# Experts: ScalarE's share of conversions and turned rows, issued one step later

## The chip, the cores and the metric

The kernel runs on one core of one Trainium2 chip. The metric is the device time of one launch, in microseconds (us). Of the core's engines five matter: TensorE (PE; its weight loads are listed as PEld), VectorE (DVE), ScalarE (ACT), GpSimd (POOL) and SyncE (SP). Each works through a queue of its own in order. DMAs are issued from the queues of SP, ScalarE and POOL.

## What is computed

Three layers follow each other: a decayed attention, a mixture of eight experts in which every token goes to one expert, and a dense layer with its own nonlinearity.

```python
def _moe_ref(x, modality_id, w_gate, modality_bias, w1, w2):
    ...
    e_idx = np.argmax(logits, axis=1)
    ...
    for e in range(E):
        mask = e_idx == e
        h = np.maximum(x[mask] @ w1[e], 0.0)
        out[mask] = gate_w[mask, None] * (h @ w2[e])

def _moe2_ref(x, w_in, w_out):
    h = x @ w_in
    g = h - np.tanh(h)
    return (g @ w_out).astype(np.float32)
```

There are 4608 tokens of 512 numbers; `w1` and `w2` have 8 x 512 x 1024, `w_in` and `w_out` 512 x 2048. The dense layer's weights come as 64-bit numbers in the kernel's eyes and are turned into 32-bit pairs on the chip.

## The kernel before

All matrix products split each factor into a rounded part and its remainder: ScalarE rounds (a copy into the type fp32r), VectorE subtracts, and TensorE adds three products (high by high, high by low, low by high).

The experts run from 154 to 606 us. Tokens are sorted by expert and cut into 12 *units* of 400; a unit has 8 *steps*, f = 0 to 7, one for each 128 of the 1024 hidden columns. `blocks` emits a step i as follows. TensorE does the first product into `hp` (12 matmuls, line 712). `post` follows: ScalarE rounds the result to `hi` (line 822), VectorE makes the rest `lo` (823); then `split_w` splits two halves of raw weights, ScalarE `wh` (790) and VectorE `wl` (791): the half for this step's second product, and the half for the first product two steps on. Then `prep` emits what else is due, and at last TensorE does the second product of step i - 2 (12 matmuls in four quarters, lines 933 to 935) into four accumulators `acc`. When that was the last of a unit, which is so at f = 1 of the next unit, `finish` has ScalarE copy the four accumulators to `yo` (912). The next unit's second product, at f = 2, starts in the same accumulators.

`prep` fits in two kinds of other work:

- *Turned rows.* The rows of the unit after this one have been gathered by POOL (line 194, 13 gathers a unit). At f = 2 to 5 VectorE turns a group of blocks (`turn_blocks`, line 169) and ScalarE rounds it to `xh` (`split_high`, 182); at f = 3 to 6 VectorE makes `xl` (`split_low`, 186) of the group before.
- *Conversions.* The 32 blocks of `w_in` and `w_out` are taken apart from 64 bit by `conv`, in pieces on VectorE: p0 and p1 (lines 221 to 223), p2 (227, 228), p3 (232, and the sum `cv_a` in 235, which ScalarE then rounds in line 236) and p4 (the low part, 240). Pieces have a price in the table `COST`; every step adds 240 to a credit, turned rows take 69 each, and pieces are issued while the credit pays for them, a p3 as the last of its step, and none at f = 1. With p3 goes the save of the conversion before (line 247, a DMA on ScalarE's queue, for `w_out` only), with p4 the load of the raw block after the next (line 212, on ScalarE's queue too).

So where ScalarE's part of a conversion or of turned rows is emitted, it stands in ScalarE's queue behind this step's `hi` and `wh` and ahead of the next step's.

Of the kernel before, what the change touches and what calls it, by code (L numbers as in the profile page):

```python
# [8 lines left out]
F32 = mybir.dt.float32  # L9
# [50 lines left out]
COST = 126, 111, 138, 69  # L60
# [55 lines left out]
def kernel(tc, A, out):  # L116
    nc = tc.nc
    with ExitStack() as ctx:
# [88 lines left out]
        def conv(cv, src, dh=None, dl=None, dst=None, bufs=2):  # L207
# [22 lines left out]
            def p3():  # L230
                lo, e = d["raw"][:, :, 0], d["e"]
                nc.vector.scalar_tensor_tensor(out=e.bitcast(F32), in0=lo.bitcast(U32), scalar=2.0 ** -52, in1=e.bitcast(F32), op0=ALU.mult, op1=ALU.mult)

                af, ef = (d[n].bitcast(F32) for n in "ae")
                nc.vector.tensor_tensor(out=af, in0=af, in1=ef, op=ALU.add)  # L235
                nc.scalar.copy(out=high(), in_=af)
# [12 lines left out]
            return load, [(COST[0], lambda: (p0(), p1())), (COST[1], p2), (COST[2], p3), (COST[3], p4)], save  # L249

        with tc.manual_schedule():
# [496 lines left out]
            with ExitStack() as c2:  # L748
# [69 lines left out]
                def post(i, hp, ht):  # L818
# [6 lines left out]
                    split_w((i, 1), (i + 2, 0))  # L825
                    load_raw(i + F1)
                    if steps[i] in ((0, 0), (0, 1)):
                        for f in range(3 * i + 3, min(F1, 3 * i + 6)):
                            load_raw(f)

# [9 lines left out]
                def swap():  # L840
# [12 lines left out]
                    for f in range(len(cvs2)):  # L853
                        fill2.extend(cvs2[f][1])
                        if f > 0:
                            fill2[-2] = (fill2[-2][0], lambda a=fill2[-2][1], b=cvs2[f - 1][2]: (a(), b()))
                        if f + 2 < len(cvs2):
                            fill2[-1] = (fill2[-1][0], lambda a=fill2[-1][1], b=cvs2[f + 2][0]: (a(), b()))
                    fill2.reverse()

                def prep(u, f):
# [18 lines left out]
                    if 0 < u < UMIN - 1:  # L880
# [4 lines left out]
                        if f in range(2, 2 + SE):  # L885
                            turn_blocks(v, f - 2, xg[v])
                            split_high(v, f - 2, xg[v])
                            credit[0] -= TURN[0]
# [13 lines left out]
                    while fill2 and fill2[-1][0] <= credit[0] and not (f == 1 and fill2[-1][0] == COST[2]):  # L902
# [6 lines left out]
                def finish(u, acc):  # L909
# [3 lines left out]
                    yos[u] = yo  # L913
                    if u == "t" or u == UMIN - 1:
                        store(u)
# [36 lines left out]
                while fill2:  # L952
                    fill2.pop()[1]()
                total = nc.values_load(nreg[0:1, 0:1], min_val=0, max_val=UMAX)
# [111 lines left out]
```

## Time and profile before

| | |
|---|---|
| time, median of 3 runs | 1397.6 us (1397.01 to 1399.13) |
| the profiled execution | 1397.72 us, of it 1396.0 from the first to the last instruction (the span) |
| TensorE busy | 1358.1 us, 97% of the span |
| VectorE busy | 1048.7 us, 75% |
| ScalarE busy | 695.9 us, 50% |
| POOL busy | 337.3 us, 24% |
| first product of the experts, first matmul | 154.1 us |
| dense layer, first matmul | 606.2 us, 789.8 before the end |

The page lists busy time by engine, the span in 40 slices, DMA queues, the chain of work that ended last and the costliest groups of instructions. Its trace can be asked for waits (who waited for whom), for groups in a stretch, and for instructions in order of time; an instruction's row gives its start, its duration, its line and its tiles, and in brackets the idle time of its engine before it and what ended that.

### The profile page before, as it was taken

To read this page: it belongs to the slowest core of one execution; us is meant where nothing else is said; L and a number is where in the kernel's file an instruction comes from. 1 tells how busy PE (TensorE), PEld (TensorE's weight loads), DVE (VectorE), ACT (ScalarE), POOL (GpSimd) and SP (SyncE) were. 2 spreads that over 40 slices of the span, in tenths; PEclk is the share of its full clock that TensorE was granted. 3 is DMA by queue.
4 is the path that set the end of the run, shared out by engine and by line. 5 is a ranking of instruction groups with operands and counts; after the bars stand their busy time and mean duration, and the time that the engine had idled before them with its cause. 6 is when DMAs were issued, how large, how long until landed. Compare 5 with 4: busy or idle time off the path is not lost.

```text
span 1396.0 us, 22342 instructions
## 1 busy us (share of the span) xinstructions
PE 1358.1 (97%) x8267; PEld 1185.8 (85%) x8267; DVE 1048.7 (75%) x1684; ACT 695.9 (50%) x1232; POOL 337.3 (24%) x381
## 2 busy tenths in 40 slices
PE   8999899999989999999999999999999999999998
PEld 7887798999989999988888888888888888888886
DVE  5766677888888888658878778787787877778775
ACT  3323444444434444446656555555555555565553
POOL 4555353343334444010011100111001110011101
PEclk9999999999999999999999999999999999999999
DMA  9997647444743336634000000000000000000000
GB/s 372 404 332 280 207 151 210 125 132 137 221 126 94 95 94 165 119 128 154 31 31 31 31 1 31 31 31 31 1 31 31 31 31 0 31 31 0 31 1 31
DMA packets 79858, 141.06 MB, mean 101 GB/s; under 512 B 36224, under 2 KB 42944, under 8 KB 79744
## 3 DMA queue, kind: packets, MB, share of 16 engines
q1 hardware_dynamic: 58912, 84.23, 19.3%
q10 hardware_dynamic: 12096, 35.45, 7.2%
q0 software_dynamic: 8736, 19.90, 4.5%
q8 instruction: 66, 1.08, 0.3%
q14 instruction: 48, 0.39, 0.1%
HBM read 133.33 MB, written 39.80 MB: 124 GB/s over the span
## 4 chain that ended last, share of the span: by engine, by line
PE 51%; issue 5%; POOL 0%; POOLq 0%; ACT 0%
PE hp L712 26%; PE acc L1010 8%; PE acc L1012 8%; PE acc L1011 8%; POOL out_dram L1036 0%; POOLq L1062 0%; ACT o L1033 0%; POOL nopt L1035 0%; POOLq L1026 0%; POOLq L1036 0%
## 5 line engine op out<-in xcount | busy, mean ns | idle before, releaser
L983 ACT ACTIVATE eh<-hp 128x512 f32<-128x512 f32 x144 | 86.4, 600 | 293.0 <-PE hp L712 276.0
L712 PE MATMUL hp<-xh,winh 128*128 128x512 f32 x576 | 224.2, 389 | 0.1
L1010 PE MATMUL acc<-wout,hi 128*128 128x512 f32 x576 | 224.2, 389 | 0.0
L1012 PE MATMUL acc<-wout,lo 128*128 128x512 f32 x576 | 224.2, 389 | 0.0
L1011 PE MATMUL acc<-wout,hi 128*128 128x512 f32 x576 | 224.1, 389 | 0.0
L712 PE MATMUL hp<-xh,winl 128*128 128x512 f32 x576 | 224.1, 389 | 0.0
L712 PE MATMUL hp<-xl,winh 128*128 128x512 f32 x576 | 224.1, 389 | 0.0
L985 DVE TENSOR_TENSOR el<-eh,hp 128x512 f32<-128x512 f32 x144 | 99.1, 688 | 156.4 <-ACT eh L984 156.4
L194 POOL DMA_INDIRECT xg<-x_d,idt x130 | 155.6, 1197 | 216.8 <-DVE cv_a L235 70.5
L740 POOL TENSOR_TENSOR xl<-yr,xh 128x512 fp32r<-128x512 f32 x36 | 49.2, 1367 | 429.7 <-ACT xh L739 429.7
L933 PE MATMUL acc<-hi,wh 128*128 128x400 f32 x384 | 132.6, 345 | 16.3 <-ACT yo L912 16.3
L994 DVE SCALAR_TENSOR_TENSOR el<-eh,el 128x512 f32<-128x512 f32 x144 | 128.5, 893 | 15.4 <-DVE el L993 0.5
L712 PE MATMUL hp<-xh,wl 128*128 128x400 f32 x384 | 133.2, 347 | 4.3 <-DVE wl L791 4.0
L791 DVE TENSOR_TENSOR wl<-raw,wh 128x1024 fp32r<-128x1024 f32 (+1 forms) x98 | 117.7, 1202 | 24.4 <-ACT wh L790 23.0
L712 PE MATMUL hp<-xh,wh 128*128 128x400 f32 x384 | 131.7, 343 | 1.2 <-ACT wh L790 0.7
L712 PE MATMUL hp<-xl,wh 128*128 128x400 f32 x384 | 131.5, 342 | 0.8 <-DVE xl L163 0.8
L934 PE MATMUL acc<-lo,wh 128*128 128x400 f32 x384 | 131.3, 342 | 0.0
L935 PE MATMUL acc<-hi,wl 128*128 128x400 f32 x384 | 131.3, 342 | 0.0
L712 PEld LDWEIGHTS hp<-xh,winh 128*128 128x128 f32 x576 | 108.2, 188 | 22.9 <-issue 0.5
L1012 PEld LDWEIGHTS acc<-wout,lo 128*128 128x128 f32 x576 | 108.1, 188 | 22.8 <-DVE lo L989 0.4
L1011 PEld LDWEIGHTS acc<-wout,hi 128*128 128x128 f32 x576 | 108.2, 188 | 22.5
L712 PEld LDWEIGHTS hp<-xh,winl 128*128 128x128 f32 x576 | 108.1, 188 | 22.6
(169 smaller groups left out, 2541.4 us busy)
## 6 DMA issues: line engine op xcount, KB each, us to landing
raw<-in_w_dram SPq DMA_DIRECT2D x91, 512.0 KB
qk<-in_qk_dram SPq DMA_DIRECT2D x36, 512.0 KB
vk<-in_vk_dram SPq DMA_DIRECT2D x36, 512.0 KB
y_d<-yo SPq DMA_DIRECT2D x12, 800.0 KB
yr<-y_d SPq DMA_DIRECT2D x9, 1024.0 KB
raw<-in_wo_dram ACTq DMA_DIRECT2D x16, 512.0 KB
wo_d<-cv_em ACTq DMA_DIRECT2D x16, 512.0 KB
raw<-in_wi_dram ACTq DMA_DIRECT2D x16, 512.0 KB
```

The lines of the kernel that those rows point to most:

```text
L194: nc.gpsimd.indirect_dma_start(out=dst, out_offset=None, in_=x_d[0:NT, :].rearrange("t (q c) -> (t q) c", q=NQ), in_offset=bass.IndirectOf ...
L712: nc.tensor.matmul(out=hp, lhsT=lhs, rhs=rhs, start=j == 0, stop=j == 3 * KD - 1)
L791: nc.vector.tensor_tensor(out=wl[:, 0:n], in0=r, in1=wh[:, 0:n].bitcast(F32), op=ALU.subtract)
L933: nc.tensor.matmul(out=o, lhsT=wh[:, cs], rhs=hi, start=first, stop=False)
L934: nc.tensor.matmul(out=o, lhsT=wh[:, cs], rhs=lo, start=False, stop=False)
L935: nc.tensor.matmul(out=o, lhsT=wl[:, cs], rhs=hi, start=False, stop=last)
L983: nc.scalar.activation(out=u, in_=hp, func=ACTF.Square)
L985: nc.vector.tensor_tensor(out=v, in0=u, in1=hp, op=ALU.mult)
L994: nc.vector.scalar_tensor_tensor(out=v, in0=s, scalar=SQ_C, in1=v, op0=ALU.add, op1=ALU.mult)
L1010: nc.tensor.matmul(out=acc[s], lhsT=hi, rhs=wh, start=first, stop=False)
L1011: nc.tensor.matmul(out=acc[s], lhsT=hi, rhs=wl, start=False, stop=False)
L1012: nc.tensor.matmul(out=acc[s], lhsT=lo, rhs=wh, start=False, stop=last)
```

## The change

ScalarE's rounding of a conversion (now `cast`, line 238), the load of the raw block after the next, the save, and `split_high` are no longer emitted where VectorE's piece is. They are put in a list, `late_act`, and `flush` emits the list in the next step's `post`, behind that step's `hi` and `wh`. At f = 1 of every unit but the first, `flush` is left to `finish`, behind the four `yo`. The cast and the load go with p3, the save with p4 of the same conversion. At f = 1 it is now p4 that isn't issued, where it was p3. No instruction is added or taken away.

```diff
--- before.py
+++ after.py
@@ -233,7 +233,9 @@
 
                 af, ef = (d[n].bitcast(F32) for n in "ae")
                 nc.vector.tensor_tensor(out=af, in0=af, in1=ef, op=ALU.add)
-                nc.scalar.copy(out=high(), in_=af)
+
+            def cast():
+                nc.scalar.copy(out=high(), in_=d["a"].bitcast(F32))
 
             def p4():
                 low = dl if dst is None else d["m"].bitcast(F32R)
@@ -246,7 +248,7 @@
                 if dst is not None:
                     nc.scalar.dma_start(out=dst, in_=d["em"].bitcast(F32))
 
-            return load, [(COST[0], lambda: (p0(), p1())), (COST[1], p2), (COST[2], p3), (COST[3], p4)], save
+            return load, [(COST[0], lambda: (p0(), p1())), (COST[1], p2), (COST[2], p3), (COST[3], p4)], cast, save
 
         with tc.manual_schedule():
             c1, c1r = ExitStack(), ExitStack()
@@ -823,10 +825,18 @@
                     nc.vector.scalar_tensor_tensor(out=lo, in0=hp, scalar=0.0, in1=hi.bitcast(F32), op0=ALU.max, op1=ALU.subtract)
                     ht[i] = (hi, lo)
                     split_w((i, 1), (i + 2, 0))
+                    if steps[i][1] != 1 or steps[i][0] == 0:
+                        flush()
                     load_raw(i + F1)
                     if steps[i] in ((0, 0), (0, 1)):
                         for f in range(3 * i + 3, min(F1, 3 * i + 6)):
                             load_raw(f)
+
+                late_act = []
+
+                def flush():
+                    while late_act:
+                        late_act.pop(0)()
 
                 def store(u):
                     row = val(u, 2)
@@ -852,10 +862,9 @@
                     cvs2.extend(conv(cv2, A["wi"][f], winh[:, f], winl[:, f]) for f in range(F3))
                     for f in range(len(cvs2)):
                         fill2.extend(cvs2[f][1])
-                        if f > 0:
-                            fill2[-2] = (fill2[-2][0], lambda a=fill2[-2][1], b=cvs2[f - 1][2]: (a(), b()))
-                        if f + 2 < len(cvs2):
-                            fill2[-1] = (fill2[-1][0], lambda a=fill2[-1][1], b=cvs2[f + 2][0]: (a(), b()))
+                        nxt = cvs2[f + 2][0] if f + 2 < len(cvs2) else lambda: None
+                        fill2[-2] = (fill2[-2][0], lambda a=fill2[-2][1], b=cvs2[f][2], c=nxt: (a(), late_act.extend((b, c))))
+                        fill2[-1] = (fill2[-1][0], lambda a=fill2[-1][1], b=cvs2[f][3]: (a(), late_act.append(b)))
                     fill2.reverse()
 
                 def prep(u, f):
@@ -884,7 +893,7 @@
                             credit[0] -= TURN[1]
                         if f in range(2, 2 + SE):
                             turn_blocks(v, f - 2, xg[v])
-                            split_high(v, f - 2, xg[v])
+                            late_act.append(lambda v=v, s=f - 2: split_high(v, s, xg[v]))
                             credit[0] -= TURN[0]
                     while pend and cvs2:
                         load_raw(pend.pop(0))
@@ -899,7 +908,7 @@
                     if u == 0 and f in (3, 4):
                         cvs2[f - 3][0]()
                     credit[0] = min(credit[0], 330)
-                    while fill2 and fill2[-1][0] <= credit[0] and not (f == 1 and fill2[-1][0] == COST[2]):
+                    while fill2 and fill2[-1][0] <= credit[0] and not (f == 1 and fill2[-1][0] == COST[3]):
                         c, piece = fill2.pop()
                         credit[0] -= c
                         piece()
@@ -911,6 +920,7 @@
                     for c in range(4):
                         nc.scalar.copy(out=yo[:, c], in_=acc[c][:, 0:UE])
                     yos[u] = yo
+                    flush()
                     if u == "t" or u == UMIN - 1:
                         store(u)
 
@@ -951,6 +961,7 @@
                 run_units(range(UMIN), None)
                 while fill2:
                     fill2.pop()[1]()
+                    flush()
                 total = nc.values_load(nreg[0:1, 0:1], min_val=0, max_val=UMAX)
 
                 with tc.If(total > UMIN):
```

The order of ScalarE in steps 0 and 1 of a unit (the eighth; `winh<-cv_a` is the conversion's rounding, `raw<-in_wi_dram` the load of a raw block). Before:

```order
L822 ACTIVATE hi<-hp 128x400
L790 CAST wh<-raw 128x1024
L236 CAST winh<-cv_a 128x512
L822 ACTIVATE hi<-hp 128x400
L790 CAST wh<-raw 128x1024
L212 DMA raw<-in_wi_dram 128x1024
L912 COPY yo<-acc 128x400 x4
```

After, the same two steps:

```order
L824 ACTIVATE hi<-hp 128x400
L792 CAST wh<-raw 128x1024
L238 CAST winh<-cv_a 128x512
L212 DMA raw<-in_wi_dram 128x1024
L824 ACTIVATE hi<-hp 128x400
L792 CAST wh<-raw 128x1024
L921 COPY yo<-acc 128x400 x4
L238 CAST winh<-cv_a 128x512
L212 DMA raw<-in_wi_dram 128x1024
```

The rounding stood ahead of step 1's `hi`; now `hi` and `wh` of step 1 come first and the four `yo` next, and a second rounding, that of a sum made in step 1, stands behind them.

The order of ScalarE in steps 2 and 3 of that unit (`xh<-xg` rounds turned rows). Before:

```order
L822 ACTIVATE hi<-hp 128x400
L790 CAST wh<-raw 128x1024
L182 CAST xh<-xg 128x4x128
L236 CAST winh<-cv_a 128x512
L822 ACTIVATE hi<-hp 128x400
L790 CAST wh<-raw 128x1024
L182 CAST xh<-xg 128x4x128
```

After:

```order
L824 ACTIVATE hi<-hp 128x400
L792 CAST wh<-raw 128x1024
L824 ACTIVATE hi<-hp 128x400
L792 CAST wh<-raw 128x1024
L182 CAST xh<-xg 128x4x128
L824 ACTIVATE hi<-hp 128x400
L792 CAST wh<-raw 128x1024
L182 CAST xh<-xg 128x4x128
```

The first `xh` has moved from the end of step 2 to behind `hi` and `wh` of step 3, and the second from step 3 to step 4; the conversion's rounding of step 2 has gone from there to step 1.

The order of VectorE in steps 0 and 1 of that unit, from behind step 0's `wl` (`winl` is p4, lines 221 to 228 are p0 to p2, 232 and 235 are p3). Before:

```order
L232 SCALAR_TENSOR_TENSOR cv_em<-raw,cv_em 128x512
L235 TENSOR_TENSOR cv_a<-cv_a,cv_em 128x512
L823 SCALAR_TENSOR_TENSOR lo<-hp,hi 128x400
L791 TENSOR_TENSOR wl<-raw,wh 128x1024
L240 TENSOR_TENSOR winl<-cv_a,winh 128x512
L221 TENSOR_SCALAR cv_em<-raw 128x512
L222 TENSOR_SCALAR cv_em<-cv_em 128x512
L223 TENSOR_SCALAR cv_a<-cv_em 128x512
L227 SCALAR_TENSOR_TENSOR cv_a<-raw,cv_a 128x512
L228 TENSOR_SCALAR cv_em<-cv_a 128x512
```

After:

```order
L242 TENSOR_TENSOR winl<-cv_a,winh 128x512
L221 TENSOR_SCALAR cv_em<-raw 128x512
L222 TENSOR_SCALAR cv_em<-cv_em 128x512
L223 TENSOR_SCALAR cv_a<-cv_em 128x512
L227 SCALAR_TENSOR_TENSOR cv_a<-raw,cv_a 128x512
L228 TENSOR_SCALAR cv_em<-cv_a 128x512
L825 SCALAR_TENSOR_TENSOR lo<-hp,hi 128x400
L793 TENSOR_TENSOR wl<-raw,wh 128x1024
L232 SCALAR_TENSOR_TENSOR cv_em<-raw,cv_em 128x512
L235 TENSOR_TENSOR cv_a<-cv_a,cv_em 128x512
```

The p3 of step 0 and the six instructions p4 to p2 of step 1 have changed places: the six now stand in step 0, and p3 in step 1.

## Rows read from the trace of the kernel before

**Rows 1.** The page, section 2: granted TensorE clock in 40 slices of the span.
```profile
PEclk9999999999999999999999999999999999999999
```

**Rows 2.** Waits, 154 to 606 us: who waited for whom, total us, times, longest.
```profile
DVE lo L823 <- ACT hi L822: 58.6, 53, 3.1
...
DVE wl L791 <- ACT wh L790: 23.0, 65, 0.5
...
PE acc L933 <- ACT yo L912: 16.3, 10, 1.6
...
DVE cv_em L221 <- DMA wo_d<-cv_em: 6.0, 4, 2.6
...
PE hp L712 <- DVE wl L791: 4.0, 3, 2.4
...
PE hp L712 <- DVE xl L163: 0.8, 1, 0.8
```

**Rows 3.** Timeline of TensorE at two switches of units: start, duration, what, idle before.
```profile
428.78 0.34 PE L712 MATMUL hp<-xh,wl 128*128 128x400 f32 x1
430.76 0.45 PE L933 MATMUL acc<-hi,wh 128*128 128x400 f32 x1 [1.64 <-ACT yo L912]
431.05 0.34 PE L934 MATMUL acc<-lo,wh 128*128 128x400 f32 x1
...
463.50 0.34 PE L712 MATMUL hp<-xl,wh 128*128 128x400 f32 x1
463.87 0.45 PE L712 MATMUL hp<-xh,wl 128*128 128x400 f32 x1
...
467.58 0.45 PE L933 MATMUL acc<-hi,wh 128*128 128x400 f32 x1 [1.64 <-ACT yo L912]
```

**Rows 4.** Busy time of each engine in one unit (instructions), clock, DMA share, GB/s.
```profile
430.76:467.58 36.82, 35.16 (x192) 34.40 (x192) 30.66 (x49) 16.28 (x28) 15.76 (x14) 1.00 0.33 91
```

**Rows 5.** Groups in that unit: VectorE, then ScalarE: busy, mean ns, idle before.
```profile
L791 DVE TENSOR_TENSOR wl<-raw,wh 128x1024 fp32r<-128x1024 f32 x9 | 11.0, 1223 | 2.2 <-ACT wh L790 2.1
L823 DVE SCALAR_TENSOR_TENSOR lo<-hp,hi 128x400 fp32r<-128x400 f32 x8 | 4.6, 571 | 3.8 <-ACT hi L822 3.8
...
L790 ACT CAST wh<-raw 128x1024 fp32r<-128x1024 f32 x8 | 8.4, 1047 | 0.0
L822 ACT ACTIVATE hi<-hp 128x400 fp32r<-128x400 f32 x8 | 4.0, 505 | 0.0
...
L182 ACT CAST xh<-xg 128x512 fp32r<-128x512 f32 (+1 forms) x4 | 2.1, 529 | 11.0 <-DVE xg L169 11.0
L236 ACT CAST winh<-cv_a 128x512 fp32r<-128x512 f32 x3 | 1.9, 622 | 9.6 <-DVE cv_a L235 9.6
```

**Rows 6.** Timeline of ScalarE at the first of the two switches.
```profile
428.36 0.62 ACT L236 CAST winh<-cv_a 128x512 fp32r<-128x512 f32 x1 [6.12 <-DVE cv_a L235]
...
430.21 1.68 ACT L912 COPY yo<-acc 128x400 f32<-128x400 f32 x4
```

**Rows 7.** Timeline of VectorE, steps 1 and 2 of the same unit.
```profile
429.41 0.57 DVE L823 SCALAR_TENSOR_TENSOR lo<-hp,hi 128x400 fp32r<-128x400 f32 x1 [1.09 <-ACT hi L822]
...
434.72 0.57 DVE L823 SCALAR_TENSOR_TENSOR lo<-hp,hi 128x400 fp32r<-128x400 f32 x1
```

**Rows 8.** Timeline: ScalarE's queue issues a save, and VectorE waits for its landing.
```profile
229.09 0.33 ACTq L247 DMA_DIRECT2D wo_d<-cv_em  x1
...
235.47 0.43 DVE L221 TENSOR_SCALAR cv_em<-raw 128x512 int32<-128x512 int32 x1 [2.56 <-DMA wo_d<-cv_em]
```

**Rows 9.** Gathers: the page's group; one row each of POOL and VectorE; landing times.
```profile
L194 POOL DMA_INDIRECT xg<-x_d,idt x130 | 155.6, 1197 | 216.8 <-DVE cv_a L235 70.5
...
472.30 1.77 POOL L194 DMA_INDIRECT xg<-x_d,idt  x1 [0.30 <-DMA xg<-x_d,idt]
...
483.42 0.70 DVE L169 STREAM_TRANSPOSE xg<-xg 128x512 f32<-128x512 f32 x1
...
DMA to landing us min/median/max: 2.4/3.3/6.4
```

## The prediction

> **What bounds the kernel now.** I read the granted clock first: full in every slice [rows 1], so no time is hidden in TensorE's clock and an idle microsecond of TensorE is one microsecond. Then the waits of the experts stretch, 154 to 606 us, because the edit touches nothing else. TensorE's largest wait there is 16.3 us in 10 pieces, all alike, for the copies `yo` of the finished accumulators; then come 4.0 us in 3 for `wl`, the low part of a weight, and 0.8 us for `xl` [rows 2]. The dense layer behind it (from 606 us) shows no such wait and isn't touched, so its length stays.
>
> Next, one unit of experts in order of time. Between two first matmuls of the second product, 430.76 and 467.58, lie 36.82 us [rows 3] and 192 matmuls [rows 4]. Undisturbed, TensorE starts one every 0.1803 us: from 431.05 to 463.50 there are 180 starts in 32.45 us [rows 3]. 192 of those are 34.61 us, so a unit loses 2.21 us. Where: the `yo` wait makes a distance of 1.98 us (428.78 to 430.76), 1.80 over the normal, and the matmul behind a stop comes 0.11 late (430.76 to 431.05); a wait for `wl` adds 0.19 (463.50 to 463.87) and again 0.11 [rows 3].
>
> Who is the pacemaker? Not TensorE: in that unit ScalarE's eight `hi` never wait, their idle is 0.0 [rows 5], so `hp` has always long been done when ScalarE comes to it. VectorE waits for ScalarE (`lo` for `hi` 3.8 us, `wl` for `wh` 2.2) and ScalarE for VectorE (11.0 us for turned rows, 9.6 for the conversion's sum) [rows 5]. These two wait for each other by turns, and TensorE pays at the unit's end. The place: `winh` (line 236) stands in ScalarE's queue ahead of the next step's `hi` and has waited 6.12 us for VectorE's sum `cv_a` [rows 6]. Behind it in a row come `hi`, `wh` and only then the first `yo` at 430.21 [rows 6], though the accumulators were complete before the last first-product matmul at 428.78 [rows 3]. VectorE meanwhile stands still for 1.09 us, until `hi` is there [rows 7].
>
> **The change part by part.** It adds and removes no instruction; it changes ScalarE's order, and VectorE's through the rule at f = 1.
>
> 1. *The cast behind `hi`, `wh` and, at a unit's second step, behind `yo`.* With nothing foreign ahead of them, `hi`, `wh` and the first `yo` are due right behind their matmuls. The first `yo` needs the first quarter of the second product of step 1; TensorE asks for it 12 first-product matmuls plus three quarters later, 3.8 us, and the four copies together take 1.68 [rows 6]. So the whole `yo` wait goes: 10 x (1.80 + 0.11) = **19.1 us**.
>
> 2. *The `wl` waits.* VectorE loses 58.6 us in the stretch to `hi` and 23.0 to `wh` [rows 2]. In the unit it needs 36.82 - 3.8 - 2.2 = 30.8 us of its own [rows 4, 5], against TensorE's 34.61. So TensorE becomes the pacemaker with 3.8 us of room per unit. One old pattern stays in each unit: a conversion's sum at step 1 is cast in that same step, ahead of the `hi` of step 2, and costs VectorE about 1.09 for `hi` [rows 7] and 0.35 for `wh` (23.0 in 65 pieces [rows 2]) again; 2.3 us are left. VectorE's longest step, six conversion instructions with `lo` and `wl`, is 5.31 us (429.41 to 434.72 [rows 7]); it now stands in step 0 and overruns TensorE's step of 24 x 0.1803 = 4.33 by 1.0 at most. How late may it be? `wl` of a step is wanted two steps later: its chain (12 matmuls, then 0.51, 1.05, 1.22) ends some 5.3 us into its step and is asked for at 8.65 + 0.36 = 9.0. Spare: 3.7 us, against a lateness of 1.0 + 1.1. So these waits go too: 4.0 us of idle in 3 pieces, 0.17 + 0.11 more for each, 4.8; and six of the kind of 463.87, 0.30 each, 1.8. Together **6.6 us**.
>
> 3. *The `xl` wait before unit 1.* The cast of step 6 of unit 0 now follows the `hi` and `wh` of step 7, ahead of the transposed rows' copy. All five still end earlier than with the cast first: **1.0 us** (0.75 + 0.17 + 0.11 by the same rule).
>
> 4. *Turned rows.* `split_high` runs one step later; `split_low` of the same rows stands in that next step behind `wl`. ScalarE does it right after `wh`, while VectorE works 1.22 us on `wl` [rows 5]; a copy of 0.53 on average [rows 5] is hidden by that. Without this cover it would be some 0.5 us a piece for VectorE, 2.1 us a unit, just inside the 2.3 us of part 2.
>
> 5. *DMAs that move.* The load of the next raw weights goes with the cast; its buffer was read last by the sum just before, and its user is two steps off. The save of a converted piece moves ahead, to the step behind the low part. A buffer's next use waited 6.0 us in 4 pieces for a save [rows 2]; the longest took from 229.09 to 235.47, 6.4 us [rows 8]. New, the save leaves behind the `yo` of step 1 and the buffer is wanted late in step 2, some 6 us on where it was 3.7. At worst the longest old wait (2.6) comes back in each of 4 units: with 1.6 us of spare left, 1 us each, 4 us. At best 0. I take 0.5 in all.
>
> 6. *POOL and SP.* Their order doesn't change. The eleventh of a unit's 13 gathers starts at 472.30 and takes 1.77; the twelfth follows 0.30 later, takes 1.20 on average and lands 3.3 us after that (median), at 478.9; the turn that reads it starts at 483.42 [rows 9]. VectorE comes earlier by no more than the 2.2 us that the unit shrinks, so 2.3 remain; one unit whose gather starts late may lose some: 0.5.
>
> Sum: 19.1 + 6.6 + 1.0 = 26.7 at most; I leave 0.5 for the saves, 0.5 for a late gather, 0.5 for the `xl` place, so **25.2**. The profiled execution took 1397.72 us (span 1396.0), 0.1 over the median: 1397.7 - 25.2 = **1372.5 us**.
>
> **The rivals.** *(a) Only the `yo` waits go.* A save or VectorE's order in step 0 (`winl`, then five more) keeps `wl` late, as at 463.87 today. For it: VectorE's long step moved, it did not shrink. Against: 3.7 us of spare. It gives 1397.7 - 19.1 - 1.0 = 1377.6.
>
> *(b) VectorE becomes the bound.* It would have to need 10% more for the same work, 33.9 + 1.45 = 35.4 us a unit. For: it is at 30.66 busy of 36.82 and would be at 89% of 34.61. Against: no instruction is added. Each unit is then 0.8 over 34.61, ten of them 8 us: 1380.
>
> *(c) The gathers starve.* A gather takes 1.20 us on average, some 1.77 [rows 9]. If VectorE, denser by 6%, held all of them to 1.77, the twelfth would come 11 x 0.57 = 6.3 us later, and the turn would wait 6.3 - 2.3 = 4.0. Of the spare of 3.7 us part 2's lateness has used up to 2.1, so TensorE would stop 2.4 us in a unit, and nearly all is lost: in ten units 24 us, 1396.5. The Trainium skill, "SBUF — State Buffer" (on the "DVE blocks DMA" trap), says that a VectorE operation that holds the port pair it shares with GpSimd keeps GpSimd from writing the descriptors of its DMAs. The trace agrees as far as a gather's time varies by half beside VectorE's work [rows 9]. Against: VectorE's work per unit is the same, and most gathers ran at full speed beside it at 83% busy.
>
> *(d) It doesn't do what it says*: the cast of the last step before a switch holds ScalarE in step 0 just as it does now in step 1. Then 1397.7 too.
>
> *(e) Slower.* At step 1 the cast stands behind four `yo`, waits for the sum that VectorE makes last in that same step, and has the `hi` of step 2 behind it. If the sum came X late, `wl` of step 2 would be X late, and TensorE would stop at step 4 for X - 3.7 in each unit. From X = 5.9 on that is more than the 2.2 saved; at X = 7 it is 1.1 us a unit more than now: 1397.7 + 11 = 1408. Against: X comes out as 1 to 2 us above.
>
> **How the numbers follow.** Forecast 0.80, (a) 0.08, (b) 0.05, (c) 0.02, (d) 0.02, (e) 0.03. The range runs from everything gone with a fast execution, 1397.7 - 26.7 - 1.0 = 1370, past (a) up to (b), 1379; what is left out, (b) to (e), is 0.12. Faster by over 0.2% (2.8 us, about what a measurement of this kernel can tell from no change): forecast, (a), (b), 0.93. Within 0.2%: (c), (d), 0.04. Slower: (e), 0.03.
>
> **What would show it.** Part 1: no TensorE wait for `yo`, and unit starts 34.6 us apart. Part 2: `hi` waits for `hp` in nearly every step, and VectorE's wait for `hi` is TensorE's doing; no `wl` wait of TensorE. Parts 5 and 6: waits of VectorE for a save or of a turn for a gather, and whether TensorE stops two steps later. The dense layer should keep its 790 us. The forecast is wrong if units stay above 35 us; then the waits list names (a), (b) or (c) by who is waited for.

## The result and the profile after

| | before | changed |
|---|---|---|
| median of four runs in one comparison | 1397.91 us (1397.01 to 1399.13) | 1375.55 us (1372.63 to 1377.41) |
| profiled execution | 1397.72 us, span 1396.0 | 1375.19 us, span 1373.5 |
| dense layer, first matmul | 606.2 us | 583.6 us |

The ratio of the medians is 0.9839 (95% interval 0.9822 to 0.9856), 22.4 us less; 1372.5 was forecast. From 200 us of the span to the dense layer it is now 22.6 us less (406.2 before, 383.6 now); the dense layer stayed within 0.1 (789.8, now 789.9).

The lines of the code have moved by 2 to 10: the first product is L714, the second L943 to L945, `hi` L824, `lo` L825, `wh` L792, `wl` L793, `yo` L921, the cast of a conversion L238. The waits of the changed kernel, 154 to 583 us, that answer to [rows 2] (who waited for whom: us in total, times, longest):

```profile
ACT hi L824 <- PE hp L714: 187.0, 82, 3.3
...
DVE lo L825 <- ACT hi L824: 41.1, 36, 3.1
...
DVE wl L793 <- ACT wh L792: 14.6, 38, 1.3
DVE xg L169 <- DMA xg<-x_d,idt: 14.0, 5, 5.3
...
PE hp L714 <- ACT wh L792: 1.8, 1, 1.8
...
PE hp L714 <- DVE wl L793: 1.6, 2, 1.4
PE hp L714 <- DVE xl L186: 1.6, 1, 1.6
```

TensorE no longer waits for `yo` at all (16.3 us in 10 before [rows 2]), and `hi` waits for TensorE's `hp` in 82 of 96 steps: TensorE sets the pace. New is the fourth line: VectorE's turns wait for gathered rows, which they never did before. One unit, from one last `xl` to the next, by engine as in [rows 4] (length; PE, PEld, DVE, ACT, POOL busy; clock; DMA share; GB/s), and its groups as in [rows 5]:

```profile
432.87:467.43 34.56, 34.56 (x193) 34.56 (x193) 30.34 (x50) 16.37 (x27) 15.09 (x13) 1.00 0.43 99
```

```profile
L793 DVE TENSOR_TENSOR wl<-raw,wh 128x1024 fp32r<-128x1024 f32 x9 | 11.0, 1222 | 1.5 <-ACT wh L792 1.4
L825 DVE SCALAR_TENSOR_TENSOR lo<-hp,hi 128x400 fp32r<-128x400 f32 x8 | 4.6, 570 | 2.6 <-ACT hi L824 2.6
...
L824 ACT ACTIVATE hi<-hp 128x400 fp32r<-128x400 f32 x8 | 4.0, 505 | 16.6 <-PE hp L714 16.6
L182 ACT CAST xh<-xg 128x512 fp32r<-128x512 f32 (+1 forms) x4 | 2.1, 533 | 0.0
L238 ACT CAST winh<-cv_a 128x512 fp32r<-128x512 f32 x3 | 1.9, 622 | 1.6 <-DVE cv_a L235 1.6
```

TensorE is busy for all of the 34.56 us; the idle time of `hi` went from 0.0 to 16.6, that of the turned rows' copy from 11.0 to 0.0. The switch of units on ScalarE and on TensorE, answering to [rows 6] and [rows 3]:

```profile
405.67 0.62 ACT L238 CAST winh<-cv_a 128x512 fp32r<-128x512 f32 x1
408.65 0.51 ACT L824 ACTIVATE hi<-hp 128x400 fp32r<-128x400 f32 x1 [2.36 <-PE hp L714]
409.05 1.04 ACT L792 CAST wh<-raw 128x1024 fp32r<-128x1024 f32 x1
409.99 1.68 ACT L921 COPY yo<-acc 128x400 f32<-128x400 f32 x4
413.24 0.62 ACT L238 CAST winh<-cv_a 128x512 fp32r<-128x512 f32 x1 [1.57 <-DVE cv_a L235]
```

```profile
412.53 0.34 PE L714 MATMUL hp<-xh,wl 128*128 128x400 f32 x1
412.71 0.34 PE L943 MATMUL acc<-hi,wh 128*128 128x400 f32 x1
```

The four copies end at 411.67, a microsecond before TensorE comes to the accumulators, and the casts stand on either side of `hi`, `wh` and `yo`.

One unit, the eleventh, is 4.2 us longer than the others (sum of what its five late or slowed matmuls add). Its rows, in the order VectorE, TensorE, POOL's first and last gather, SyncE's save of result rows and the copy of their token numbers, which the kernel issues right behind it:

```profile
534.11 0.71 DVE L169 STREAM_TRANSPOSE xg<-xg 128x512 f32<-128x512 f32 x1 [5.33 <-DMA xg<-x_d,idt]
541.77 0.31 DVE L169 STREAM_TRANSPOSE xg<-xg 128x128 f32<-128x128 f32 x1 [3.44 <-DMA xg<-x_d,idt]
```

```profile
537.79 0.45 PE L714 MATMUL hp<-xh,wl 128*128 128x400 f32 x1 [1.44 <-DVE wl L793]
544.47 0.45 PE L714 MATMUL hp<-xl,wh 128*128 128x400 f32 x1 [1.60 <-DVE xl L186]
```

```profile
508.89 0.94 POOL L194 DMA_INDIRECT xg<-x_d,idt  x1 [18.09 <-DMA idt<-slot_d]
...
526.62 0.94 POOL L194 DMA_INDIRECT xg<-x_d,idt  x1 [0.31 <-issue]
```

```profile
525.39 0.42 SPq L843 DMA_DIRECT2D y_d<-yo  x1
526.09 0.65 SPq L844 DMA_DIRECT2D tok_d<-slot_d  x1
```

A turn waits for rows, VectorE's `wl` and `xl` are late behind it, TensorE stops. The gathers began 6.9 us after the unit's last `xl` (501.99), and the last was issued 1.2 us *behind* the save.

### The profile page after: what moved, and what is told of

The parts are those of the page before. It is cut to its first block, busy times and chain, and to the rows that moved or that the text cites. A ratio compares the mean times of both kernels' runs of the same rounds, so it can differ in the third digit from the quotient of the medians.

```text
span 1373.5 us, 22319 instructions
## 1 busy us (share of the span) xinstructions
PE 1352.7 (98%) x8267; PEld 1187.4 (86%) x8267; DVE 1043.9 (76%) x1684; ACT 696.9 (51%) x1232; POOL 331.9 (24%) x381
## 4 chain that ended last, share of the span: by engine, by line
PE 51%; issue 5%; POOL 0%; POOLq 0%; ACT 0%
PE hp L714 26%; PE acc L1021 8%; PE acc L1022 8%; PE acc L1023 8%; POOL out_dram L1047 0%; POOLq L1073 0%; ACT o L1044 0%; POOL nopt L1046 0%; POOLq L1037 0%; POOLq L1047 0%
## 5 line engine op out<-in xcount | busy, mean ns | idle before, releaser
L714 PE MATMUL hp<-xh,winh 128*128 128x512 f32 x576 | 224.2, 389 | 0.1
L714 PE MATMUL hp<-xh,winl 128*128 128x512 f32 x576 | 224.1, 389 | 0.0
L714 PE MATMUL hp<-xl,winh 128*128 128x512 f32 x576 | 224.1, 389 | 0.0
L194 POOL DMA_INDIRECT xg<-x_d,idt x130 | 151.4, 1165 | 194.6 <-issue 52.1
L824 ACT ACTIVATE hi<-hp 128x400 fp32r<-128x400 f32 x96 | 48.4, 505 | 187.0 <-PE hp L714 187.0
L714 PE MATMUL hp<-xh,wh 128*128 128x400 f32 x384 | 131.8, 343 | 2.2 <-ACT wh L792 1.8
L714 PE MATMUL hp<-xh,wl 128*128 128x400 f32 x384 | 131.8, 343 | 1.7 <-DVE wl L793 1.6
L714 PE MATMUL hp<-xl,wh 128*128 128x400 f32 x384 | 131.6, 343 | 1.8 <-DVE xl L186 1.6
L943 PE MATMUL acc<-hi,wh 128*128 128x400 f32 x384 | 131.7, 343 | 0.0
L945 PE MATMUL acc<-hi,wl 128*128 128x400 f32 x384 | 131.4, 342 | 0.0
L793 DVE TENSOR_TENSOR wl<-raw,wh 128x1024 fp32r<-128x1024 f32 (+1 forms) x98 | 117.5, 1199 | 15.9 <-ACT wh L792 14.6
L714 PEld LDWEIGHTS hp<-xh,winh 128*128 128x128 f32 x576 | 108.2, 188 | 22.9 <-issue 0.5
L1022 PEld LDWEIGHTS acc<-wout,hi 128*128 128x128 f32 x576 | 108.2, 188 | 22.5
```

The lines of the kernel that those rows point to most:

```text
L194: nc.gpsimd.indirect_dma_start(out=dst, out_offset=None, in_=x_d[0:NT, :].rearrange("t (q c) -> (t q) c", q=NQ), in_offset=bass.IndirectOf ...
L714: nc.tensor.matmul(out=hp, lhsT=lhs, rhs=rhs, start=j == 0, stop=j == 3 * KD - 1)
L793: nc.vector.tensor_tensor(out=wl[:, 0:n], in0=r, in1=wh[:, 0:n].bitcast(F32), op=ALU.subtract)
L943: nc.tensor.matmul(out=o, lhsT=wh[:, cs], rhs=hi, start=first, stop=False)
L945: nc.tensor.matmul(out=o, lhsT=wl[:, cs], rhs=hi, start=False, stop=last)
L1022: nc.tensor.matmul(out=acc[s], lhsT=hi, rhs=wl, start=False, stop=False)
```

## The experiments

Theory A, the prediction's: VectorE and ScalarE paced each other, because casts and turned rows stood ahead of the next step's `hi`; once they stand behind, TensorE alone is the pacemaker and VectorE has 2 to 3 us to spare in a unit. Rival B: only the cast ahead of `yo` is at fault, and the rest of the change does nothing. Later came theory D on the gathers. Kernels of one group ran on one chip; the chip of the first group took 1406.5 us for the kernel before (the others 1399.0 and 1399.2), so ratios to the kernel before are compared.

| kernel | median us | ratio to before, 95% |
|---|---|---|
| changed, first time | 1375.55 | 0.9839 (0.9822 to 0.9856) |
| changed, second time | 1377.59 | 0.9850 (0.9834 to 0.9867) |
| casts alone late | 1388.19 | 0.9869 (0.9847 to 0.9892) |
| turned rows alone late | 1392.40 | 0.9899 (0.9880 to 0.9919) |
| only the casts at a switch late | 1400.39 | 0.9961 (0.9947 to 0.9975) |
| lists of ids early | 1440.26 | 1.0239 (1.0191 to 1.0288) |
| `lo` twice | 1382.94 | 0.9878 (0.9838 to 0.9918) |
| `wl` twice | 1390.17 | 0.9935 (0.9916 to 0.9955) |
| load of `yr` a unit later | 1370.93 | 0.9797 (0.9780 to 0.9813) |
| two id tiles | 1380.24 | 0.9860 (0.9833 to 0.9887) |
| save in step 2 | 1377.27 | 0.9839 (0.9820 to 0.9858) |
| save in step 4 | 1369.52 | 0.9786 (0.9767 to 0.9805) |
| both late | 1370.34 | 0.9794 (0.9774 to 0.9815) |

### Only the casts at a switch

The changed kernel, with turned rows in their own step and only those casts late whose sums are made in a unit's steps 0 and 1:

```diff
-                    if steps[i][1] != 1 or steps[i][0] == 0:
-                        flush()
...
-                            late_act.append(lambda v=v, s=f - 2: split_high(v, s, xg[v]))
+                            split_high(v, f - 2, xg[v])
...
+                        if u == 0 or f > 1:
+                            flush()
```

> Late, behind the four yo, is only the cast of a sum made in steps 0 and 1 of a unit; all other casts, and the turned rows, are issued in their own step; VectorE's order is that of the changed kernel. So nothing stands ahead of yo any more. Theory A: VectorE still waits 1.45 us at three casts and 0.5 to 0.9 at rows in a unit, so a unit stays near 36.8 us and TensorE waits for wl instead of yo: 1394 to 1398 us. Rival B (the yo wait is the fault of the one cast ahead of it): the 19 us of the yo waits come back, about 1378 us.

Measured: 6 us gained of 22. Its waits, 154 to 606 us:

```profile
PE hp L714 <- DVE wl L793: 5.8, 10, 0.6
PE hp L714 <- ACT wh L792: 4.0, 10, 1.5
PE hp L714 <- DVE xl L186: 1.7, 4, 0.7
```

The wait for `yo` is gone as in the changed kernel, yet TensorE now stops for `wh` and `wl` once in each of ten units, and the units are 37.4 and later 36.3 us long. The time came back in another place, so the wait for `yo` was where the loss showed, not what caused it. B falls. A had expected a little less gain still: of the 1397.9 us before, 0.9961 is 1392.5, and A had said 1394 to 1398.

### Casts alone, turned rows alone

```diff
-                            late_act.append(lambda v=v, s=f - 2: split_high(v, s, xg[v]))
+                            split_high(v, f - 2, xg[v])
```

> The conversions' casts are late as in the changed kernel, the rounding of turned rows stays in its own step. Theory A (VectorE and ScalarE pace a unit by waiting for each other; each cast in place costs VectorE 1.09 + 0.36 us, a row's rounding only where nothing of VectorE stands between the turn and the next lo): in the new order a piece of a conversion follows each turn, so the rounding is hidden and units stay at 34.6 us: 1373 to 1377 us. Rival B (turned rows matter as much as casts, 0.5 to 0.9 us for each of four a unit): units of 35.5 or more, 1383 us or more.

The other one is the kernel before with the late list for `split_high` alone:

```diff
-                            split_high(v, f - 2, xg[v])
+                            late_act.append(lambda v=v, s=f - 2: split_high(v, s, xg[v]))
```

> Only the rounding of turned rows is late; casts stay in their step as before the change. Theory A: three casts in place keep 3 x 1.45 us of VectorE's waits, 30.8 + 4.4 + some waits for wh = about 35.6 us a unit; TensorE still stops for yo, about 0.9 us instead of 1.63, so some 1.2 us a unit less than before: 1384 to 1387 us. Rival B (the stop for yo comes only from the cast that stands ahead of it): nothing changes, 1397 us, yo waits of 1.6 us.

Casts alone gain 1.3%, rows alone 1.0%, both 1.5 to 1.6%: the parts overlap, as two ways to shorten one loop would. The two fastest runs with casts alone (1385.8 and 1386.1 us) have the 0.985 of both together, so late rows add little to late casts. With rows alone the waits for `yo` are still there but half as long (154 to 606 us):

```profile
PE acc L940 <- ACT yo L919: 8.4, 8, 2.4
```

With casts alone seven units from 273.35 to 517.98 us average 34.95 us, 0.4 more than in the changed kernel, and in its profiled execution, the slowest of the four, one late gather costs 7.6 us more (a turn waits 10.9 us for it). Rows alone agree with A. Casts alone lie between A and B: 0.9869, where A's 1373 to 1377 us are 0.982 to 0.985 and B's 1383 is 0.989, and units of 34.95 us, where A has 34.6 and B 35.5.

### How much room VectorE has

Two kernels add work to VectorE alone, in every odd step: `lo` computed twice (2.3 us more a unit), `wl` computed twice (4.9 us more). The repeated results are the same, only the work is doubled. The changed kernel ran beside them:

> The changed kernel once more, so that the other kernels of this group have it on their own chip. Every theory: its ratio to the kernel before is that of the first measurement, 0.984 within 0.003, and the units between 294 and 502 us of the span stand 34.6 us apart.

```diff
+                    if steps[i][0] not in ("t", 0) and steps[i][1] % 2:
+                        nc.vector.scalar_tensor_tensor(out=lo, in0=hp, scalar=0.0, in1=hi.bitcast(F32), op0=ALU.max, op1=ALU.subtract)
```

> The changed kernel with the remainder `lo` computed twice by VectorE in every odd step from the second unit on: four more of 0.57 us, 2.3 us of VectorE work in each unit. Theory A (after the change TensorE alone paces the experts' units, at 34.56 us, and VectorE, busy 30.3 of them, has about 4 us of room): the units stay at 34.6 to 34.9 us, the time is that of the changed kernel within 4 us. Rival (VectorE with its waits for `hi` and `wh` is the pacer now, its 4.2 idle microseconds being all waits that it can't shed): units of 36.8 us, some 11 x 2.3 = 25 us slower than the changed kernel, a ratio of about 1.001 to the kernel before.

```diff
+                        if parts[-1][1] // F1 > 0 and parts[-1][1] % 2:
+                            nc.vector.tensor_tensor(out=wl[:, 0:n], in0=r, in1=wh[:, 0:n].bitcast(F32), op=ALU.subtract)
```

> The changed kernel with the remainder `wl` of the weights computed twice by VectorE in every odd step from the second unit on: four more of 1.22 us, 4.9 us in each unit. Theory A (about 4 us of room): VectorE now needs 30.3 + 4.9 = 35.2 us of its own, more than TensorE's 34.56; the units become 35.5 to 37 us and the kernel 10 to 27 us slower than the changed one (ratio to the kernel before 0.991 to 1.003). If the units stayed at 34.6, the room would be larger than thought; if they took 39.4 (34.56 + 4.9), there would be none.

One unit of each, `lo` twice and then `wl` twice, counted from one last `xl` to the next, that is by VectorE's clock:

```profile
433.78:467.92 34.14, 34.14 (x192) 34.14 (x191) 32.07 (x53) 16.75 (x27) 15.06 (x13) 1.00 0.39 97
```

```profile
445.72:482.47 36.75, 35.63 (x194) 34.35 (x193) 34.67 (x53) 16.78 (x28) 15.92 (x13) 1.00 0.36 90
```

With `lo` twice TensorE stops only once between 262 and 530 us, for 0.1 us at 388, and otherwise starts a step every 4.32 us, the same 34.56 a unit; VectorE, late after a wait at 363 us, even catches up by 0.42 us in each unit, so its own pace with 2.28 us added is 34.14. With `wl` twice VectorE is the pacemaker: 36.75 is 34.14 and the difference of the two additions (4.9 - 2.3 = 2.6). So VectorE alone would need 31.9 us in the changed kernel, and the room is 34.56 - 31.9 = 2.7 us. The median with `lo` twice is 5.4 us over the changed kernel's, more than expected. It is no matter of pace: in its profiled execution a turn of the eleventh unit waited 11.5 us for rows, and TensorE stopped:

```profile
544.79 0.70 PE L714 MATMUL hp<-xh,wl 128*128 128x400 f32 x1 [9.47 <-DVE wl L793]
```

With `wl` twice, where the units are longer, no turn waits over 1.4 us. By TensorE's starts its units lose 21.9 us against 34.56 each in its profiled execution, 2.2 in most of them and 5.3 in the eleventh; those of the changed kernel beside it lose 7.0, all in the eleventh. The difference of 14.9 fits the 14.4 between the two executions (the medians differ by 12.6).

### The late gathers

Theory C: in the eleventh unit the first load of turned result rows (`yr`) stands on SyncE's queue, waits 8.0 us, and makes the list of ids late, and so the gathers. The condition of that load was replaced:

```diff
-                        if (u - E + 1) * UE + E - 1 >= UB and yr0[0] is None:
+                        if u == UMIN - 2 and yr0[0] is None:
```

> The changed kernel with the first load of turned result rows (yr from y_d) issued one unit later, so that it no longer stands on SyncE's queue, waiting 8.0 us, ahead of the eleventh unit's list of ids. Theory C (that wait makes the list late, the list makes the gathers late, and two turns of VectorE that wait 5.3 and 3.4 us for them cost TensorE the 4.2 us that the eleventh unit is longer): the gathers of the unit at 502 us start within 3 us of its last `xl`, no turn waits for a gather over 1 us, and the kernel is 3 to 4 us faster than the changed one. Rival (the gathers are late because the raw weights of that unit keep their queue, or their landing is slow whatever the start): the eleventh unit stays 3 to 4 us longer than the others and the time doesn't move. The later load may itself come late for the last unit's rows of y; then the last unit shows a wait for yr.

It gained more than expected, 6.7 us against the changed kernel beside it, and in its profiled execution no turn of the eleventh unit waits. But there the same stall sits in another unit, where `yr` is not loaded at all (a turn, the last gather, the save):

```profile
362.43 0.71 DVE L169 STREAM_TRANSPOSE xg<-xg 128x512 f32<-128x512 f32 x1 [7.24 <-DMA xg<-x_d,idt]
```

```profile
352.85 0.94 POOL L194 DMA_INDIRECT xg<-x_d,idt  x1 [0.30 <-issue]
```

```profile
351.61 0.43 SPq L843 DMA_DIRECT2D y_d<-yo  x1
```

So `yr` is not the cause. What the two places share: the last gather is issued 1.2 us behind the save of 800 KB of result rows. (In the eleventh unit the later `yr` put the last gather 1.5 us ahead of the save, so the gain goes by that distance too.) Theory D: rows whose packets are in flight behind that save are held up. Over the profiled executions (ten units with gathers in each), by when a unit's last gather is issued, from the save that follows its first gather:

| last gather | kernels (units) | longest wait of a turn for rows |
|---|---|---|
| 1.2 to 4.4 us behind the save | changed (2), changed again (2), casts alone (3), `lo` twice (1), `yr` later (1), two id tiles (2), save in step 2 (4) | 3.4 to 11.7 us in 14 of the 15 units, 0.8 in one |
| within 0.3 us of it | before (1), changed and five others | 0 to 2.8 us |
| 1.3 us or more ahead of it | all | at most 1.2 us |

In the kernel before the last gather was 3.7 to 7.1 us ahead in nine units and 0.1 in the tenth, and no turn waited. It isn't that the DMAs are moving much else: here is what they move in the changed kernel from 500 to 545 us, in 40 slices of 1.1 us:

```profile
GB/s 80 33 133 370 402 239 2 0 178 313 98 390 135 58 55 320 233 284 255 295 244 62 113 353 337 384 161 111 15 7 4 11 0 29 36 255 415 361 168 33
```

From 531.5 to 537 us it is nearly nothing, while twelve packets of gathers, begun 4.6 to 6.1 us behind the save (at 525.39), each take 8.8 to 9.5 us. With `lo` twice the held packets begin 4.8 to 12.8 us behind the save, and all of them end 13 to 15 us behind it, as these do. In the changed kernel's third unit a turn waits 4.1 us although no packet is that long, and with `yr` later the 7.2 us wait has no gather packet over 1.1 us; there it is packets of raw weights that take up to 4.8.

The packets of the traces also show that "the save" is two transfers, and that not only gathers are slow. `store` issues the 800 KB of rows, 512 packets of 1600 bytes, and 0.7 us behind them a copy of the unit's 400 token numbers (line 844), some 400 packets of 4 bytes. In the changed kernel's eleventh unit the 1600-byte packets take 0.07 us each (at most 0.23) and have ended 5.5 us behind the save; the 30 gather packets that begin beside them take 0.17 (at most 0.87). The packets of 4 bytes go out mostly 3.9 to 4.6 us behind the save, and the packets that are held begin from 4.6 on. Between 160 and 600 us of all fourteen profiles, the kernel before among them, 676 packets of 1600 bytes or more took over 3 us, on every queue, and each of them began 2.5 to 13 us behind the issue of such a copy; that is where 13 to 23% of such packets begin. Other saves (`wo_d`, 512 KB each) and the loads of the list of ids, also of 4 bytes a packet, have none behind them when no `store` is near. The timing points at the copy of the token numbers, but every kernel moves both transfers together, so no run tells which of the two does it.

To test D, `store` was moved a step either way, and with it, in the same block, the copy of the token numbers and the first load of `yr`:

```diff
-                    if f == 3 and u - 1 in yos:
+                    if f == 4 and u - 1 in yos:
```

> The changed kernel with the save of a unit's result rows (y_d from yo, 800 KB) issued in step 4 of the next unit instead of step 3; only SyncE's order differs, and the list of ids now stands ahead of the save. In the traces so far every long wait of a turn for its gathered rows (5.3, 7.1, 7.2, 11.5 us) is in a unit whose last gather was issued 1.2 to 2.5 us after that save, with single gather packets that take up to 9.6 us; units whose last gather is out 1 us or more before the save have none. Theory D (the save's many writes hold up gathers that are still in flight): the last gather is out before the save in every unit, no turn waits over 2 us, and the kernel is 3 to 6 us faster than the changed one, about 1372 where the changed one takes 1376. Rival (the gathers are late for another reason, such as the late list or the load of yr): the eleventh unit stays 3 to 4 us longer than the others, no difference.

(with `f == 2` for the other)

> The same save one step earlier than in the changed kernel, in step 2: some 4.3 us earlier, so that 2 to 4 of the 13 gathers of every unit are issued behind it. Theory D: gather packets of over 5 us and turns that wait 3 to 9 us in most of the ten units, each unit with one some 4 us longer, the kernel 10 to 40 us slower than the changed one. Rival (the collision isn't what delays the gathers): the time of the changed kernel within 4 us, long waits in the eleventh unit alone. The save may itself wait on SyncE for the copies of yo and hold up raw weights behind it; that would show as waits for wh or wl of raw weights.

The save in step 4 is the fastest kernel here: 1369.52 us, four runs within 1.1 us, and its interval lies below those of both measurements of the changed kernel. All of TensorE's waits in it, 154 to 583 us:

```profile
PE m L498 <- DVE oh_all L489: 1.3, 1, 1.3
PE hp L714 <- ACT wh L792: 1.2, 1, 1.2
PE m L642 <- DVE cum L512: 0.8, 1, 0.8
PE hp L714 <- DVE xl L163: 0.2, 1, 0.2
```

With the list now ahead of the save on SyncE's queue, the gathers begin half a microsecond behind the last `xl` (500.55), and the last is out 10 us ahead of the next save:

```profile
493.27 1.92 SPq L191 DMA_DIRECT2D idt<-slot_d  x4
496.03 0.43 SPq L843 DMA_DIRECT2D y_d<-yo  x1
...
527.77 0.42 SPq L843 DMA_DIRECT2D y_d<-yo  x1
```

```profile
501.04 0.94 POOL L194 DMA_INDIRECT xg<-x_d,idt  x1 [16.08 <-DVE xl L186]
...
517.82 1.70 POOL L194 DMA_INDIRECT xg<-x_d,idt  x1 [0.30 <-issue]
```

The save's effect is still there: the first gathers of each unit now meet the save of that unit, and packets begun 6 to 12 us behind it take up to 4.1 us. But those rows are wanted only at 518.6, and no turn waits. So the gain is not a hold-up that has gone but one that lies where there is time to spare. The edit does two things at once: the gathers begin earlier, and `store` comes later.

The save in step 2 did not do what was expected: no stall in most units, and the time of the changed kernel. The list of ids behind the save moved ahead with it, so the gathers also began earlier, and only four units have an overlap of 1.2 us or more; three of these wait 4.4, 6.6 and 7.7 us, the fourth 0.8. D holds for the units in which the two meet, but that edit doesn't make them meet in all. It also speaks against the rival that gathers merely begin too late: the two longest waits are in units whose gathers began 3.1 and 3.4 us behind the last `xl`, while those for the fifth to tenth unit of the changed kernel began 3.7 to 5.0 us behind it, and there a turn waits 0.5 us at most. Moving both, save and load of `yr`, gives no more:

> The changed kernel with the save in step 4 and with the first load of yr one unit later, both together. If the two act on one and the same loss (the late gathers of the eleventh unit), it is as fast as the better of them alone, 4 to 7 us under the changed kernel, about 1370; if each takes a loss of its own, up to 10 us under it.

1370.34 us, the same as either alone: they act on one loss. By what the two transfers of `store` hold packets up (in the memory, on the way there, in the queues) no run tells.

### Lists of ids early, which stays open

Before D, the list of ids itself was moved from step 4 to step 1 of the unit, with a second buffer:

```diff
-                    P["id"] = pr("id2", 1, side="right")
+                    P["id"] = pr("id2", 2, side="right")
...
-                        if (u, f) == (max(v - 2, 0), g):
+                        if (u, f) == ((v - 2, 1) if v > TURNED else (0, g)):
```

> The changed kernel, with the gather's list of token numbers loaded three steps earlier (step 1 of a unit instead of step 4, two tiles for it instead of one). Theory: in the changed kernel the gathers start 3.7 to 6.9 us behind the last xl of the rows before, since the list comes late; in the eleventh unit a turn then waits 5.3 and 3.4 us for its gather and TensorE stops 4.2 us. With the list there, gathers start within about 2 us of that xl: no such stop, 1370 to 1372 us, and runs closer together. Rival (the gathered rows land late because weights are loaded at the same time): turns wait as before, 1375 us.

It came out 2.4% *slower* than the kernel before. The gathers begin 0.5 us behind the last `xl`, as meant, and no turn waits. But at the switches ScalarE stands still for 4.6 to 11.4 us ahead of `hi`, mostly for something that the profile can only call remote, and TensorE stops some 4 us. At one of them:

```profile
410.19 0.50 ACT L824 ACTIVATE hi<-hp 128x400 fp32r<-128x400 f32 x1 [4.59 <-remote]
...
420.38 0.50 ACT L824 ACTIVATE hi<-hp 128x400 fp32r<-128x400 f32 x1 [8.23 <-remote]
```

The first products for these `hi` had their last matmul at 408.10 and 412.42. Half of the edit was then run by itself:

> The changed kernel with two buffers for the list of ids instead of one, the list still loaded in step 4: one half of the kernel with early lists that came out 2.4% slower than before. If the second buffer alone did that (through where other tiles come to lie), this one is as slow, some 30 us over the kernel before; if the early place of the load did it (gathers that begin within 0.5 us of the last xl), this one has the time of the changed kernel within 4 us, with gathers that begin 1 to 7 us behind the last xl as before.

It has about the time of the changed kernel (0.1 to 0.2% over it, intervals overlapping), with an 11.7 us wait of the kind of D. So the second buffer isn't it. The early start of the gathers isn't it either, since they start as early with the save in step 4, at no cost. What is left is the place of the list's load on SyncE's queue, in step 1 ahead of raw weights, or that together with the second buffer. Why ScalarE should go on only 2 to 8 us after these matmuls because of that, no run here shows.

## Why the prediction was right, and where it was off

**What bounds the kernel**: right. Waits moved from `yo` to `wh` and `wl` when only the switch was mended, and vanished, but for the stops of the eleventh unit, when all casts and turned rows were late.

**Part 1, the `yo` waits, 19.1 us**: right that none is left. But 19.1 us is not what that wait is worth by itself: with only the switch mended it went too, and 6.1 us came back. So the parts are not worth their waits one by one. What carries the sum is what the working says ahead of them, that VectorE and ScalarE wait for each other by turns: the change ends that in every step.

**Part 2, the `wl` waits and VectorE's room**: right. It was put at 2.3 us a unit and is 2.7 by the two kernels with added work. Units came to 34.56 us where 34.61 was taken. What is left of `wl` waits is 0.2 us at 259.59 and the 1.4 of the eleventh unit, which is the gather's.

**Part 3, `xl` before unit 1**: the wait of 0.8 us fell to 0.2, within the reserve.

**Part 4, turned rows**: in the unit shown the copy `xh` no longer waits (11.0 to 0.0), and in none does VectorE wait for it.

**Part 5, saves of converted pieces**: 0.5 us was put in; VectorE's wait for them (6.0 in 4) is gone. In the kernel with the save in step 4 it is back with 7.4 us in 5 pieces, and TensorE doesn't feel it.

**Part 6, the gathers: the step that was mis-sized.** A late gather was put at 0.5 us; in the eleventh unit it cost 4.2 us (7.0 in the second profiled execution, 11.9 with `lo` twice), and that is more than the shortfall of 2.7 us (25.2 forecast, 22.5 between the profiled executions). Without it the runs also lie closer together: 1369.2 to 1370.2 with the save in step 4, where the changed kernel has 1372.6 to 1379.3. The working looked at POOL's and SyncE's order, found it unchanged, and took the landing time as given [rows 9]. What it missed is a distance *between* two queues. On SyncE's queue the save stands behind a load of raw weights that waits for the `wl` of step 3: at the switches shown that `wl` ended at 441.59 before and at 420.57 now, the load went out at 441.62 and 420.60, the save at 442.47 and 421.45, long after the last `yo` (431.89 and 411.67). As VectorE's steps come earlier, so does the save: 22.9 us behind the end of the last `xl`, where it was 24.9. The gathers do not: they began 3.5 us behind that end, where it was 2.4. From 3.7 to 7.1 us behind the last gather (nine units of ten) it went to within 1.6 us of it on either side (seven of ten). A step that becomes earlier brings its DMAs with it.

**The rivals.** (a) is out: `wl` waits went too. (b) is out: VectorE is 2.7 us short of being the bound. (c) named the right engine for the wrong reason: gathers did starve, but not of time on POOL. They took 1.17 us on average where it was 1.20 [rows 9], and in the stalled unit all were issued by 527.6. The Trainium skill, "SBUF — State Buffer" (on the "DVE blocks DMA" trap), speaks of the writing of descriptors beside VectorE; here the delay lay behind that: twelve packets of gathers already issued took 8.8 to 9.5 us. (d) and (e) are out: the cast behind `yo` waits 1.57 us for its sum at the switch shown, and no cast of the stretch waits over 3.3, far from the 5.9 at which (e) would decide.

## What to carry to other kernels

When an engine works in order, put what waits for another engine behind the work that a third one waits for, in every step and not only where the wait shows: mending the place of the largest wait alone gave 6 of 22 us, and the rest came back as other waits. Measure the new pacemaker's room by adding work to the next engine until the time moves. And after such a change look at which transfers have come closer to each other: here a store, with the copy of a list behind it, moved a few microseconds and met the next unit's gathers, and one number in SyncE's order was worth another 7 to 9 us by the ratios (0.9839 and 0.9850 against 0.9786).

## What was not expected of the hardware

Behind a save of 800 KB and the copy of 400 numbers of 4 bytes that follows it, packets on every queue are slow for some 10 us: gather packets take up to 9.6 us each, those that are held longest until 13 to 15 us behind the save, while the DMAs move 0 to 15 GB/s.

Behind some of its stops TensorE is granted half its clock for a while, the 1.2 GHz level: matmuls start 0.333 us apart instead of 0.180. Behind the stop of 9.5 us with `lo` twice (the last three numbers are clock, DMA share, GB/s):

```profile
544.79:549.29 4.50, 4.50 (x14) 4.46 (x14) 4.40 (x10) 0.95 (x3) 0.00 (x0) 0.50 0.59 174
```

The fourteen matmuls there take 4.5 us where they would take 2.5, so the clock adds 2 us to the stop. Stops of 2.6 and 3.7 us with the save in step 2 show 0.51 and 0.50, and one of 1.8 us with `wl` twice shows 0.56 (554.56 to 558.30); the two of 1.4 and 1.6 us in the changed kernel and one of 2.4 us in the kernel before (390.22 to 392.50) left the clock at 1.00. So the length of a stop alone doesn't tell what follows. Where the clock falls, a stalled turn costs TensorE more than the stop itself: in the second profiled execution of the changed kernel some 1.7 of the 7.0 us are slow matmuls (clock 0.52 from 544.33 to 547.90). In the first the 4.2 us are stops alone.
